# Output projection: transposes of the second normalisation one step later, copies by half, residuals loaded one tile ahead

## The chip, the cores and the metric

The kernel runs on one core of a Trainium2 chip. The metric is the device time of one execution in microseconds (us), as the median of several runs; lower is better. One more execution was recorded by the profiler, and all rows shown here come from it. PE is TensorE (matmul; PEld is its weight load), DVE is VectorE, ACT is ScalarE, POOL is GpSimd, SP is SyncE, which issues all the DMAs here.

## The reference

One transformer block with modulation (adaLN): 2048 tokens, width 1024, 32 heads of 32, feed-forward width 3584.

```python
h = _layernorm(x) * (1 + ca) + sa
x = x + ga * _A_ref(h, wq, wk, wv, wo, beta)     # 4 segments of 512 tokens, softmax attention + a memory
h = _layernorm(x) * (1 + cb) + sb
x = x + gb * _B_ref(h, w_gate, w_up, w_down)     # (gelu(h @ w_gate) * (h @ w_up)) @ w_down
```

The change sits where the first half ends and the second begins: `o @ wo`, the addition of the residual `x`, and the second layer normalisation with its scale `1 + cb` and shift `sb`, whose result is wanted transposed (width on the partitions) for the feed-forward products.

## The kernel before, in words

**Stages.** An opening and 33 attention steps (until about 990 us), the output projection (from 937 us within the last two attention steps, alone until 1151.5 us), the gate and up products (`gate_up`, two passes over the tokens, 28 column blocks each) and the down product (`down`).

**Precision.** Every product of the projection and the feed-forward is done in three matmuls with operands cut into a high part (ACT copy into fp32r) and a low part (DVE or POOL subtraction): high x high, low x high, high x low. Such cuts (L201 to L208 for the attention output, L821 and L823 for the feed-forward's operands) are the most frequent work of ACT, DVE and POOL around the change.

**Output projection (`project`, L678 to L697; `projections`, L739 to L772).** Blocks of (segment s, half nb of the 1024 output columns) run in the order (0,0), (1,0), (0,1), (1,1), (2,0), (3,0), (2,1), (3,1). A block has four tiles of 128 tokens by 512 columns. A tile loads its residual from `x` (L684), issues 24 matmuls into one of two PSUM slots (`mm_ps`, L690), and after them DVE adds PSUM and residual (L694) and SP stores the sum to `x1_d` (L695). So the second tile after a tile can only start when that tile's addition has read its PSUM slot.

**Where a residual lives (`x_tile`, L665).** In the first six blocks it is one of four quarters of a buffer `xr`, taken in turn; in the blocks (2,1) and (3,1) it is half of a tile of the ring `raw`, which has four slots and serves operand loads as well: `a_part` (L951) takes two slots of it for its odd columns, `b_part` (L1018, L1019) two for each column block of the gate and up weights.

**Steps and sides.** After every six matmuls `project` yields, and `step()` gives each entry of the list `sides` one or two turns: load and cut the next segment's attention output (`load_hT`), normalise (`norm_tiles`), cut the first feed-forward operands (`a_part`, `b_part`). A tile of the projection is four such steps. Within a step the engines get the work in the order of the list. PE, DVE, ACT and POOL keep the order in which the program names their instructions. SP keeps it too during attention, that is for the block (0,0) and the first tiles of (1,0); later the planner orders SP's DMAs by its own estimate of when they are ready.

**Second normalisation (`norm_tiles` with name "b", `norm_steps`).** Eight tiles of 128 tokens by 1024 (segments 0 and 1) start five steps apart from the block (0,1) on. Counted from its own start, a tile is loaded from `x1_d` at step 0 (L238); at step 5 DVE takes its statistics (L216 to L221) and POOL the power -1/2 (L222); at step 7 DVE forms the shift (L227) and ACT scales the tile in place (L229); at steps 9 and 10 its two halves are transposed by PE, four 128 x 128 blocks into one PSUM tile (`turn`, L250), and the four blocks are copied out with scale and shift, two by ACT (L258) and two by DVE (L256) in turn, into one buffer that SP sends to `h2_d` (L259). With five steps between tiles, step 10 of one tile is step 5 of the next, and the turn comes first in it. The other eight tiles (segments 2 and 3) are normalised in the same way within the first pass of `gate_up`, with `wait=6` and spacings of their own (L271 to L287).

**First users.** `a_part((1, 6, 2, 7))` reads `h2_d` from the 11th step of the block (3,0) on, and cuts in (2,1); `a_part((5, 4))` follows in (3,1). The first product of `gate_up` runs at 1151.5 us.

Of the kernel before, what the change touches and what calls it, by code (L numbers as in the profile page):

```python
# [19 lines left out]
P = 128  # L20
# [9 lines left out]
L = 512  # L30
# [6 lines left out]
def block_kernel(ctx: ExitStack, tc: tile.TileContext, x, c, wmod, wq, wkv, wo, beta, wg, wu, wd, out):  # L37
    nc = tc.nc
# [37 lines left out]
    def raw_tile(name):  # L76
        return big.tile([P, 1024], F32, name=name, tag="raw", bufs=4)
# [4 lines left out]
    def tmp_tile(name):  # L82
        return big.tile([P, L], F32, name=name, tag="tmp", bufs=4)
# [5 lines left out]
    def mm_ps(name):  # L89
        return psum.tile([P, L], F32, name=name, tag="mm", bufs=2)  # L90

    def s_ps(name):
        return psum.tile([P, L], F32, name=name, tag="s", bufs=5)
# [118 lines left out]
    def norm_stats(halves, name, behind=False):  # L212
        st = cs([P, 2, 6], "st" + name, tag="st", bufs=4)
        mv = cs([P, 2], "mv" + name, tag="mv", bufs=4)
        for h in range(2):
            i = nc.vector.bn_stats(st[:, h], halves[h])  # L216
            if behind:
                hold(i)
        nc.vector.bn_aggr(mv, st.rearrange("p a b -> p (a b)"))
        rs = cs([P, 1], "rs" + name, tag="rs", bufs=4)  # L220
        nc.vector.tensor_scalar_add(rs, mv[:, 1:2], EPS)  # L221
        nc.gpsimd.tensor_tensor(rs, rs, mhalf[:, :1], op=ALU.pow)  # L222
        return mv, rs

    def norm_scale(ts, mv, rs, name):
        mr = cs([P, 1], f"mr{name}", tag="mr", bufs=4)
        nc.vector.tensor_scalar(mr, mv[:, 0:1], rs, -1.0, op0=ALU.mult, op1=ALU.mult)  # L227
        for t in ts:
            nc.scalar.activation(t, t, AF.Identity, bias=mr, scale=rs)  # L229

    def norm_tiles(src, dst, segs, jscale, jshift, name, tiles=range(4), wait=0, get=raw_tile, more=[]):

        toks = [s * L + i * P for s in segs for i in tiles] + more
        dv = dst.rearrange("(k p) t -> p k t", p=P)
        xs = {}
        def load(q):
            xs[q] = (raw_tile if name == "b" and not wait and q % 3 == 2 else get)(f"n{name}{toks[q]}")
            nc.sync.dma_start(xs[q], src[toks[q]:toks[q] + P, :])  # L238

        def stat(q):  # L240
            t = xs[q]
            xs[q, "s"] = norm_stats([t[:, :L], t[:, L:]], f"{name}{toks[q]}")

        def turn(q, h):
            t, tok = xs[q], toks[q]
            ps = s_ps(f"tp{name}{tok}_{h}")
            hh = tmp_tile(f"ht{name}{tok}_{h}")
            for k in range(4):
                kt = 4 * h + k
                nc.tensor.transpose(ps[:, k * P:(k + 1) * P], t[:, kt * P:(kt + 1) * P], ident)  # L250
            for k in range(4):
                kt = 4 * h + k
                sl = slice(k * P, (k + 1) * P)
                sc, sh = (modT[:, 8 * j + kt:8 * j + kt + 1] for j in (jscale, jshift))
                if h if name == "a" else k % 2:
                    nc.vector.tensor_scalar(hh[:, sl], ps[:, sl], sc, sh, op0=ALU.mult, op1=ALU.add)  # L256
                else:
                    nc.scalar.activation(hh[:, sl], ps[:, sl], AF.Identity, bias=sh, scale=sc)  # L258
            send_h = lambda: nc.sync.dma_start(dv[:, 4 * h:4 * h + 4, tok:tok + P], hh.rearrange("p (k t) -> p k t", t=P))  # L259
            if wait:  # L260
                later(3, send_h)
            elif name == "a":
                xs[q, h] = send_h
            else:
                send_h()

        if name == "a":
            return load, lambda q: stat(q), lambda q: norm_scale([xs[q]], *xs.pop((q, "s")), f"a{toks[q]}"), turn, lambda q, h: xs.pop((q, h))()
        return norm_steps(toks, xs, load, turn, name, wait)

    def norm_steps(toks, xs, load, turn, name, wait):  # L271
        if wait:
            for q in range(len(toks)):
                load(q)
                for _ in range(wait):
                    yield
                t, nm = xs[q], f"{name}{toks[q]}"
                mv, rs = norm_stats([t[:, :L], t[:, L:]], nm)
                for _ in range(3):
                    yield  # L280
                norm_scale([t], mv, rs, nm)
                for _ in range(wait - 2):
                    yield
                for h in range(2):
                    turn(q, h)
                    yield
            return  # L287
        for at in range(5 * len(toks) + 7):
            for q in range(len(toks)):
                k = at - 5 * q  # L290
                if k == 0:
                    load(q)
                elif k == 5:
                    t, nm = xs[q], f"{name}{toks[q]}"
                    st = norm_stats([t[:, :L], t[:, L:]], nm)
                elif k == 7:
                    norm_scale([t], *st, nm)
                elif k in (9, 10):
                    turn(q, k - 9)
            yield  # L300

    def norm_seg(s, halves):
# [34 lines left out]
    for n in range(2):  # L337
        k = p1.tile([P, 4, L], F32R, name=f"ks{n}")
# [326 lines left out]
    def x_tile(name):  # L665

        if xrs[0] is None:
            return raw_tile(name)[:, :L]
        xrs[1] += 1
        return f32(xrs[0][:, xrs[1] // 2 % 2, xrs[1] % 2 * L:(xrs[1] % 2 + 1) * L])  # L670
# [5 lines left out]
        return r  # L676

    def project(s, todo):  # L678
        for i, nb in todo:
            ws = wot[nb]  # L680
            tok = s * L + i * P
            fs = slice(nb * L, (nb + 1) * L)
            xr = x_tile(f"xr{s}_{nb}_{i}")
            nc.sync.dma_start(xr, x[tok:tok + P, fs])  # L684
            ps = mm_ps(f"y{s}_{nb}_{i}")
            for g in range(G):
                w = ws[g // 2].rearrange("p h (k m) -> p h k m", m=L)
                hi, lo = oh[s][g]
                for a, b in ((0, hi), (0, lo), (1, hi)):
                    nc.tensor.matmul(ps, b[:, i * P:(i + 1) * P], w[:, a, g % 2],  # L690
                                     start=(g == 0 and a == 0 and b is hi), stop=(g == G - 1 and a == 1))
                if g % 2 == 1 and g < G - 1:
                    yield
            nc.vector.tensor_add(xr, ps, xr)  # L694
            store = lambda tok=tok, fs=fs, xr=xr: nc.sync.dma_start(x1_d[tok:tok + P, fs], xr)  # L695
            later(2, store) if waiting[0] else store()
            yield  # L697
# [4 lines left out]
    def later(n, f):  # L702

        late.append([n, f])
# [34 lines left out]
    def projections():  # L739
        def block(s, *nbs):  # L740
            for _ in project(s, [(i, nb) for i in range(4) for nb in nbs]):
                step()
                yield
# [934 lines left out]
```

## Time and profile before

| | |
|---|---|
| time, median of 3 runs | 2776.51 us (2775.17 to 2778.23) |
| the profiled execution | 2774.08 us |
| its span, first to last instruction | 2772.4 us |
| mean granted TensorE clock | 0.995 |
| PE busy | 2725.8 us (98%) |
| PEld, DVE, ACT, POOL busy | 82%, 57%, 43%, 32% |
| HBM traffic | 372.79 MB read, 211.81 MB written |
| share of L690 (output projection) in the chain that ended last | 4% |

How to read it: a row of a group gives line, engine, operation and tiles, then the count and the times; buffer numbers are left out of names. "a <- b: t, n, m" among the waits says that a waited for b for t us in n times, m at the longest. In a list in order of time the columns are start, length, engine, line, operation, count, and in brackets the idle time of the engine before it with what ended it. A wait for several things is put down to the one that came last; where that one had long been done, it was another, often a DMA. `nb` are the tiles of the second normalisation, `tpb` their transposes in PSUM, `htb` the copies, `xr` a residual, `y` the projection's sums, `ra`, `rb` and `A` the feed-forward's left operands, `rg`, `ru` and `B` its right ones.

### The profile page before, as it was taken

The numbers are of one execution on the slowest core, as the hardware profiler recorded it, in microseconds if no ns is written. First come the engines' busy times: TensorE is split into PE (matmuls) and PEld (weight loads), VectorE is DVE, ScalarE is ACT, GpSimd is POOL, SyncE is SP. The second block draws the span as 40 slices with busy tenths as digits, with TensorE's granted clock in tenths as the row PEclk, the third lists the DMA queues.
The fourth block names the chain that finished last, engine by engine and source line by source line (L and its number), as shares of the span: only waits on it lengthen the run. The fifth ranks groups of instructions, "written<-read, shape, count | busy, mean of one in ns | idle before, by whom it ended". The sixth has DMA issues, their size and how long they took to land.

```text
span 2772.4 us, 43014 instructions
## 1 busy us (share of the span) xinstructions
PE 2725.8 (98%) x14748; PEld 2286.4 (82%) x14748; DVE 1568.4 (57%) x3519; ACT 1204.0 (43%) x2806; POOL 888.9 (32%) x1448
## 2 busy tenths in 40 slices
PE   7999999999999999999999999999999999999999
PEld 6798888888888777778888878888888888888887
DVE  7677667766676735655555445333433244475456
ACT  5677777776767624334322323111111033233323
POOL 5333334533333533344555552444351000000000
PEclk8999999999999999999999999999999999999999
DMA  6455444435443558778898778999999687796563
GB/s 228 135 147 151 113 145 137 134 100 147 121 130 100 149 183 273 243 293 302 321 340 322 267 267 279 341 362 362 353 361 329 215 303 264 259 307 207 179 206 127
DMA packets 244890, 637.77 MB, mean 230 GB/s; under 512 B 24768, under 2 KB 49344, under 8 KB 244672
## 3 DMA queue, kind: packets, MB, share of 16 engines
q1 hardware_dynamic: 244672, 635.03, 67.5%
q8 instruction: 116, 1.90, 0.3%
q14 instruction: 102, 0.84, 0.1%
HBM read 372.79 MB, written 211.81 MB: 211 GB/s over the span
## 4 chain that ended last, share of the span: by engine, by line
PE 89%; DVE 4%; issue 2%; POOL 2%; DMA 1%; ACT 1%; SPq 0%; POOLq 0%; ACTq 0%; DVEq 0%
PE f L1107 35%; PE y L1306 19%; PE kv L367 12%; PE q L373 6%; PE y L690 4%; PE S L524 3%; PE T L615 3%; PE O L627 3%; PE num L583 1%; PE M L566 1%; PE tpb L250 0%; POOL t L827 0%; PE R L633 0%; PE kT L401 0%; PE kv L496 0%
## 5 line engine op out<-in xcount | busy, mean ns | idle before, releaser
L1107 PE MATMUL f<-A,B 128*128 128x512 f32 x4704 | 1075.0, 390 | 3.6 <-DVE c L1127 1.5
L1107 PEld LDWEIGHTS f<-A,B 128*128 128x128 f32 x4704 | 880.8, 188 | 190.8 <-DVE c L1119 2.8
L1306 PE MATMUL y<-B,L 128*128 128x512 f32 x2352 | 533.3, 389 | 0.0
L1306 PEld LDWEIGHTS y<-B,L 128*128 128x128 f32 x2352 | 441.4, 188 | 91.7
L528 ACT ACTIVATE sj<-sj,mm 128x384 f32<-128x384 f32 (+3 forms) x512 | 281.4, 552 | 52.6 <-DVE mm L526 52.0
L526 DVE CUSTOM_DVE_ANT_0 sj<-S,mask 128x384 f32<-128x384 f32 (+3 forms) x512 | 227.9, 488 | 109.7 <-PE S L524 85.5
L618 POOL TENSOR_SCALAR_AFFINE_SELECT pt<-pt 128x128 f32<-128x128 f32 x512 | 165.3, 345 | 295.0 <-ACT pt L617 288.4
L821 ACT ACTIVATE L<-X 128x512 fp32r<-128x512 f32 x168 | 105.8, 630 | 258.6 <-PE y L1306 167.9
L617 ACT ACTIVATE pt<-T 128x256 f32<-128x256 f32 (+3 forms) x512 | 182.0, 445 | 66.0 <-PE T L615 58.8
L367 PE MATMUL kv<-w,hhh 128*128 128x256 f32 x1024 | 199.6, 285 | 0.0
L823 DVE TENSOR_TENSOR L<-X,L 128x512 fp32r<-128x512 f32 x168 | 116.0, 692 | 146.2 <-ACT L L821 146.1
L1130 ACT ACTIVATE g<-g 128x512 f32<-128x512 f32 x56 | 35.3, 631 | 339.9 <-DVE g L1129 339.9
L358 POOL TENSOR_TENSOR w<-r,w 128x256 fp32r<-128x256 f32 x180 | 133.1, 771 | 155.3 <-ACT w L352 153.7
L367 PE MATMUL kv<-w,hha 128*128 128x256 f32 x896 | 177.0, 285 | 0.0
L1046 POOL TENSOR_TENSOR rw<-rw,gbb 128x256 f32<-128x256 f32 x112 | 91.6, 853 | 247.4 <-DMA rw<-wd 166.5
L367 PEld LDWEIGHTS kv<-w,hhh 128*128 128x128 f32 x1024 | 164.8, 191 | 1.4 <-issue 0.4
L367 PEld LDWEIGHTS kv<-w,hha 128*128 128x128 f32 x896 | 145.6, 191 | 2.0 <-issue 0.8
L367 PE MATMUL kv<-w,hlh 128*128 128x256 f32 x512 | 144.7, 283 | 0.0
L690 PE MATMUL y<-wo,hho 128*128 128x512 f32 x384 | 125.7, 394 | 1.7 <-DVE xr L694 1.7
L367 PE MATMUL kv<-w,hla 128*128 128x256 f32 x448 | 126.9, 283 | 0.0
L1123 ACT ACTIVATE g<-f 128x512 f32<-128x512 f32 x56 | 33.5, 598 | 206.5 <-PE f L1107 206.5
L615 PE MATMUL T<-qs,ks 128*128 128x256 f32 (+2 forms) x512 | 108.3, 334 | 7.5 <-DVE qs L543 4.6
(244 smaller groups left out, 4215.4 us busy)
## 6 DMA issues: line engine op xcount, KB each, us to landing
bc_d<-B SPq DMA_DIRECT2D x189, 512.0 KB, 5.4
B<-bc_d SPq DMA_DIRECT2D x189, 512.0 KB, 5.4
B<-wc_d SPq DMA_DIRECT2D x112, 512.0 KB, 3.8
hid_d<-g SPq DMA_DIRECT2D x56, 512.0 KB, 4.3
wc_d<-T SPq DMA_DIRECT2D x56, 512.0 KB, 7.0
X<-hid_d SPq DMA_DIRECT2D x112, 256.0 KB, 4.9
wr<-gd_d SPq DMA_DIRECT2D x84, 256.0 KB, 4.0
ks<-kh SPq DMA_DIRECT2D x64, 256.0 KB, 3.6
```

The source lines that it names most:

```text
L358: nc.gpsimd.tensor_sub(w[:, 1, c], r[:, c], f32(w[:, 0, c]))
L367: nc.tensor.matmul(ps, b[:, sl], w[:, a], start=(kt == 0 and a == 0 and b is hi), stop=(kt == KT - 1 and a == 1), **kw)
L373: nc.tensor.matmul(ps, w[:, a], b, start=(kt == 0 and a == 0 and b is hi), stop=(kt == KT - 1 and a == 1), **kw)
L526: nc.vector.tensor_tensor_reduce(out=sj[:, :nv], in0=ps[:, :nv], in1=mask[:, L - nv:], scale=-1.0, scalar=3.4e38, op0=ALU.add, op1=ALU.min ...
L528: nc.scalar.activation(sj[:, :nv], sj[:, :nv], AF.Exp, bias=mm[:, j, i:i + 1], scale=-1.0, accum_out=ll[:, i, j:j + 1])
L615: nc.tensor.matmul(ps[:, :nn], ks[:, j, kc * P:(kc + 1) * P], qs[:, j, L - nn:], start=True, stop=True)
L617: nc.scalar.activation(pt, ps[:, nn - n:nn], AF.Exp)
L618: nc.gpsimd.affine_select(pt[:, :P], pt[:, :P], pattern=[[1, P]], compare_op=ALU.is_ge, fill=0.0, base=0, channel_multiplier=-1)
L690: nc.tensor.matmul(ps, b[:, i * P:(i + 1) * P], w[:, a, g % 2], start=(g == 0 and a == 0 and b is hi), stop=(g == G - 1 and a == 1))
L823: eng.tensor_sub(lo[:, k], src[:, k], f32(hi)[:, k])
L1107: nc.tensor.matmul(ps, B[m, i][:, a, kt * P:(kt + 1) * P], A[p, i, kt][b], start=(start and kt == 0 and a == 0 and b == 0), stop=(kt == 3 ...
L1306: nc.tensor.matmul(banks[t], ops[k][:, y, t * P:(t + 1) * P], B[slots[k]][:, x], start=(i not in (2, 4, 3) and j == 0 and x == 0 and y == ...
```

## The change

Three edits:

- In `turn`, which half goes to which engine: the four copies of half 0 are all done by ACT, the four of half 1 all by DVE. Before, that held for the first normalisation (name "a") only, and for "b" even blocks went to ACT and odd ones to DVE. The "b" tiles within `gate_up` go through the same lines.
- In `norm_steps`, the branch without `wait`: the halves are turned at steps 10 and 11 instead of 9 and 10, and the loop is one step longer.
- In `project`, the load of a residual: at a block's start the loads of its first two tiles are asked for, and at the start of each further tile that of the tile after it. Before, each tile asked for its own.

```diff
-                if h if name == "a" else k % 2:
+                if h:
                     nc.vector.tensor_scalar(hh[:, sl], ps[:, sl], sc, sh, op0=ALU.mult, op1=ALU.add)
                 else:
                     nc.scalar.activation(hh[:, sl], ps[:, sl], AF.Identity, bias=sh, scale=sc)
...
-        for at in range(5 * len(toks) + 7):
+        for at in range(5 * len(toks) + 8):
...
-                elif k in (9, 10):
-                    turn(q, k - 9)
+                elif k in (10, 11):
+                    turn(q, k - 10)
...
     def project(s, todo):
-        for i, nb in todo:
+        ahead = []
+
+        def load(i, nb):
+            ahead.append(x_tile(f"xr{s}_{nb}_{i}"))
+            nc.sync.dma_start(ahead[-1], x[s * L + i * P:s * L + (i + 1) * P, nb * L:(nb + 1) * L])
+
+        load(*todo[0])
+        for n, (i, nb) in enumerate(todo):
             ws = wot[nb]
             tok = s * L + i * P
             fs = slice(nb * L, (nb + 1) * L)
-            xr = x_tile(f"xr{s}_{nb}_{i}")
-            nc.sync.dma_start(xr, x[tok:tok + P, fs])
+            xr = ahead.pop()
+            if n + 1 < len(todo):
+                load(*todo[n + 1])
             ps = mm_ps(f"y{s}_{nb}_{i}")
```

With the turn at steps 10 and 11, step 10 of one tile is still step 5 of the next; now the first half is turned in it, ahead of the next tile's statistics in the program, and the second half one step after them.

## The prediction

> **What bounds the kernel now.** I read the page first, then the table by stretch, then who waited for whom on PE, then the lists in order of time around single waits.
>
> ```profile
> PE 2725.8 (98%) x14748; PEld 2286.4 (82%) x14748; DVE 1568.4 (57%) x3519; ACT 1204.0 (43%) x2806; POOL 888.9 (32%) x1448
> ```
> ```profile
> 1000.00:1100.00 100.00, 95.75 (x448) 77.58 (x448) 46.97 (x101) 36.68 (x64) 26.62 (x36) 1.00 0.72 233
> 1100.00:1152.00 52.00, 50.26 (x222) 41.09 (x221) 30.80 (x45) 12.92 (x23) 11.97 (x12) 1.00 0.85 276
> 1200.00:1400.00 200.00, 197.07 (x891) 160.50 (x890) 116.30 (x195) 77.27 (x137) 103.50 (x130) 1.00 0.84 306
> ```
> PE sets the end: it is busy for 2725.8 of the 2772.4 us, and everything that the change touches can only pay by filling PE's gaps. The columns of the table are length, busy time of PE, PEld, DVE, ACT, POOL, the granted clock, DMA share, GB/s. In the output projection (until 1151.5 us) PE idles 4.3 and 1.7 us in the first two rows, and 2.9 us in the 200 us of feed-forward in which the second half of the tiles is normalised. That is all there is to win. Who holds PE there:
>
> ```profile
> PE tpb L250 <- ACT nb L229: 4.3, 7, 1.1
> PE y L690 <- DVE xr L694: 1.7, 1, 1.7
> PE f L1107 <- DVE c L1119: 1.0, 3, 0.6
> ```
> Seven times the transposes wait for the scaling of their tile, once a projection waits for a PSUM slot that an old tile's residual addition (L694) still holds; in the feed-forward stage products wait for VectorE evictions such as L1119.
>
> **The transposes, part one.** One of the seven waits, on PE, then DVE and ACT:
>
> ```profile
> 1046.02 0.60 PE L250 MATMUL tpb<-ident,nb 128*128 128x128 f32 x4
> ...
> 1051.70 0.39 PE L690 MATMUL y<-ks,hho 128*128 128x512 f32 x1
> 1052.84 0.66 PE L250 MATMUL tpb<-ident,nb 128*128 128x128 f32 x4 [0.76 <-ACT nb L229]
> ...
> 1054.49 0.39 PE L690 MATMUL y<-ks,hho 128*128 128x512 f32 x1
> 1054.73 0.60 PE L250 MATMUL tpb<-ident,nb 128*128 128x128 f32 x4
> ```
> ```profile
> 1048.13 0.41 DVE L256 TENSOR_SCALAR htb<-tpb,modT 128x128 f32<-128x128 f32 x1 [0.53 <-ACT htb L258]
> 1048.46 1.28 DVE L216 BATCH_NORM_STATS2 stb<-nb 128x6 f32<-128x512 f32 x2
> 1050.10 0.69 DVE L694 TENSOR_TENSOR xr<-y,xr 128x512 f32<-128x512 f32 x1
> 1050.70 0.68 DVE L208 TENSOR_TENSOR hlo<-ro,hho 128x512 fp32r<-128x512 f32 x1
> 1051.30 0.21 DVE L227 TENSOR_SCALAR mrb<-mvb,rsb 128x1 f32<-128x1 f32 x1
> ```
> ```profile
> 1051.55 1.24 ACT L229 ACTIVATE nb<-nb,mrb,rsb 128x1024 f32<-128x1024 f32 x1 [2.92 <-DVE mrb L227]
> ```
> Read as a loop: the second half of one tile is transposed at 1046.02; its copies ping-pong between ACT and DVE until 1048.54; only then does DVE, in its order, take the next tile's statistics, POOL the power, DVE the mean and ACT the scaling, done at 1052.79, 6.77 us after 1046.02. PE would come to the next tile's first half at 1051.70 + 0.24 = 1051.94, 5.92 us after (0.24 is the undisturbed step from a projection to a transpose, 1054.49 to 1054.73). So it waits: 1052.84 - 1051.94 = 0.90 us, the shown idle of 0.76 and 0.14 beside it. Seven such: 4.3 + 7 x 0.14 = **5.3 us**; the shown 4.3 is the lower end.
>
> The change alters this loop twice. First, with the transposes one step later (six matmuls, some 1.4 us: the halves start 1054.73 - 1052.84 = 1.89 us apart, of which the four transposes take about 0.5), the next tile's statistics stand in the step of the *first* half, one ahead of the second. Second, copies by half take DVE out of the first half, so the statistics no longer wait for a transpose at all. The longest wait, 1.1 + 0.14, is shorter than the step alone. What is late next: the second half's four copies now stand ahead of the mean on DVE. From the second half's transposes on: 0.66 for these, 4 x 0.41 of copies, in the worst alignment one cut (0.68) and one residual addition (0.69), the mean 0.21, the scaling 1.24: 5.1 us, against 5.92 on PE. Some 0.3 to 0.6 of hand-overs still fit. I take **-5.3 us**; ends 0 (the loop stays) and -5.3.
>
> **Copies by half.** Nothing is added: eight copies of a tile remain four on each engine.
>
> ```profile
> L258 ACT ACTIVATE htb<-tpb,modT x64: 437/458/461, 1027.9 to 1365.8; 128x128 f32<-128x128 f32 x64
> L256 DVE TENSOR_SCALAR htb<-tpb,modT x64: 399/410/413, 1028.4 to 1366.3; 128x128 f32<-128x128 f32 x64
> ...
>   DVE htb L256: 38.9, 51
> ```
> The last row: DVE sat idle 38.9 us in 51 waits for ACT's copy of the same PSUM tile, so the two take turns although they write different columns. By half, an engine needs 4 x 0.41 to 0.46 = 1.6 to 1.8 us without a partner. In the feed-forward stage the same chain stands ahead of evictions:
>
> ```profile
> 1281.03 16.62 PE L1107 MATMUL f<-A,B 128*128 128x512 f32 x72 [0.63 <-DVE c L1119]
> 1368.18 22.05 PE L1107 MATMUL f<-A,B 128*128 128x512 f32 x96 [0.87 <-DVE c L1125]
> ```
> ```profile
> 1279.17 0.41 DVE L256 TENSOR_SCALAR htb<-tpb,modT 128x128 f32<-128x128 f32 x1 [0.53 <-ACT htb L258]
> 1279.68 0.69 DVE L823 TENSOR_TENSOR B<-rg,B 128x512 fp32r<-128x512 f32 x1
> 1280.30 0.68 DVE L1119 TENSOR_TENSOR c<-f,c 128x512 f32<-128x512 f32 x1
> ...
> 1366.31 0.41 DVE L256 TENSOR_SCALAR htb<-tpb,modT 128x128 f32<-128x128 f32 x1 [0.53 <-ACT htb L258]
> ```
> Before 1281.03 about one hand-over (0.53) goes, so some 0.5 of the 0.63. Before 1368.18 the cut between the halves comes first and all four copies (1.64) after it, where now two and a hand-over stand (2 x 0.41 + 0.53), so it stays or grows by 0.3. On balance **-0.4 us** over the stage; ends -1.5 (both waits) and +1.5 (ACT's four in a row push an eviction as far again the other way).
>
> **The residual, loaded one tile ahead.** Only one wait hangs on it:
>
> ```profile
> 1118.93 0.79 SPq L951 DMA_DIRECT2D ra<-h_d  x2
> ...
> 1120.87 0.83 SPq L684 DMA_DIRECT2D xr<-x  x1
> ```
> ```profile
> xr<-x SPq DMA_DIRECT2D x1, 256.0 KB, 7.7
> ```
> ```profile
> 1123.88 0.68 DVE L969 TENSOR_TENSOR s<-ra,s 128x512 f32<-128x512 f32 x1
> 1128.68 0.69 DVE L694 TENSOR_TENSOR xr<-y,xr 128x512 f32<-128x512 f32 x1 [4.12 <-PE y L690]
> 1129.29 0.68 DVE L823 TENSOR_TENSOR A<-ra,A 128x512 fp32r<-128x512 f32 x1
> ...
> 1134.28 0.68 DVE L694 TENSOR_TENSOR xr<-y,xr 128x512 f32<-128x512 f32 x1
> ```
> ```profile
> 1127.31 0.39 PE L690 MATMUL y<-ks,hho 128*128 128x512 f32 x1
> 1129.43 0.50 PE L690 MATMUL y<-wo,hho 128*128 128x512 f32 x1 [1.74 <-DVE xr L694]
> ```
> The idle of 4.12 is booked on PE, but the load issued at 1120.87 needs 7.7 us and lands at 1128.6, just ahead of the addition: it is the load. The Trainium skill, "DMA: Bandwidth & Descriptors", section "Anatomy of one DMA — SWDGE (gpsimd) path", fits one DMA (of another issue path) with about 2.0 us plus its bytes at 436 GB/s, which makes an estimate of 2.6 us for these 256 KB. By that it would have landed at 1123.5, the wait would have another cause, and the edit would be worth nothing; the row of 7.7 us speaks against the fit in this stretch. PE loses 2.12 - 0.24 = **1.9 us**. The new load is asked for a tile earlier, but takes a slot of the four-slot ring `raw`, which until 1118.9 belongs to operand tiles and residuals in flight. So I expect it some 2 us earlier, ahead of the two operand loads of 1118.93 instead of behind them; even with 7.7 us to landing its addition is then over by 1127.3, when PE comes for the slot (1127.31 + 0.24), and DVE is free from 1124.56. What is late next: from 1129.29 to 1134.96 DVE does one operand column and then the next tile's addition, 5.67 us, which must end by 1129.43 - 1.9 + 5.5 = 1133.0 (a tile is four steps); it may start up to 1127.3, and the operand's ScalarE cut is done at 1125.9 (row below). Slack 1.4 us, and a load of 256 KB more ahead of it costs about 1 us at the 276 GB/s of this stretch. I take **-1.9**; ends 0 and -1.9.
>
> ```profile
> 1125.23 0.63 ACT L821 ACTIVATE A<-ra 128x512 fp32r<-128x512 f32 x1 [2.46 <-DMA ra<-h_d]
> ```
> Costed at nothing: the other 31 residual loads, as many and as large as before, only earlier on SP. On SP each moves ahead of stores and tile loads, and waits for its slot:
>
> ```profile
> SPq L684 <- DMA x_d<-xr: 25.7, 11, 4.8
> ```
> ```profile
> 1043.47 0.33 SPq L238 DMA_DIRECT2D nb<-x_d  x1
> 1057.20 1.28 DVE L216 BATCH_NORM_STATS2 stb<-nb 128x6 f32<-128x512 f32 x2
> ```
> Behind it wait the tiles to normalise; one is issued some 14 us before use (last two rows), so 4.8 us more is covered. Without that cover each such wait would come back as a wait of L216.
>
> **Sum.** -5.3 - 0.4 - 1.9 = **-7.6 us**. The profiled execution took 2774.08 us (span 2772.4 and 1.7 around it), 2.4 under the median of the runs shown; the sum is against its own gaps, and its result there is 2766.5. Moved to the median, 2776.51 - 7.6 = **2768.9 us**. A measurement of this kernel can tell about 0.2%, 5.6 us, from no change: the forecast is just beyond that.
>
> **Rivals.** (1) *The residual arrives no earlier*, since its slot comes free only with the operand tiles and DMA is 0.85 busy there: then 5.7 is won, **2770.8**. For it: the slot; against: the load now stands ahead of two 512 KB loads. (The fit of the Trainium skill, above, would give the same time for another reason.) (2) *The loop closes again*: the four DVE copies of the second half, a cut and an addition fall together more often than I think, and half of the 5.3 stays: -4.9, **2771.6**. (3) *The ring turns against it*, the slower case: residuals now hold a `raw` slot one tile longer, and the last pair of operand loads (1118.93) gets the slot of the residual asked for ahead of it. That one is added at 1125 to 1126, done 0.7 later, and stored in about the 7.7 us that its load took, so the operand loads go out up to 15.4 us late (1134.3); past the slack of 1.4 us each us is PE's, at the second tile of the last block: +14.0 on the -7.6, **2782.9**. It decides at an operand load issued after about 1128 in the old time, where the gain is gone. Against: today the pair found its two slots free at 1118.93, before this residual asked for one.
>
> **Chances.** Forecast 58%, rival 1 14%, rival 2 and mixtures of both 20%, rival 3 8%. Rivals 1 and 2 lie about the bound of 2771.0, so of their 34% some 12 count as faster: faster 70%, same 22%, slower 8%. The range runs from 2765.5 (both eviction waits gone too, and 1.5 us of spread of the runs) to 2775.5 (a small part of the loop gain only); rival 3 and little else lies outside.
>
> **What would show it.** Right: no PE wait for nb L229; the waits of DVE htb on ACT htb gone; statistics (L216) starting before the second half's copies; the residual of 1120.87 issued ahead of the operand pair, and no wait of PE on L694. Wrong: a tpb wait on nb with mrb released late; operand loads (L951) later than 1119 by more than 1.4 us against the projection; new waits of f on A or c.

## The result and the profile after

The changed kernel takes **2764.85 us** (median of 5 runs, 2762.92 to 2765.96), the kernel before 2776.54 beside it (5 runs, 2775.17 to 2778.23). The ratio is 0.9956, with a 95% interval of 0.9941 to 0.9971: 11.7 us faster, where 7.6 were forecast, and 0.65 us below the lower end of the range. The profiled execution of after took 2764.85 us (span 2763.1), 9.2 less than that of before.

The page's engine line, and the same three stages as before, moved to where they now lie (length, then busy time of PE, PEld, DVE, ACT, POOL, clock, DMA share, GB/s):

```profile
PE 2725.3 (99%) x14748; PEld 2288.7 (83%) x14748; DVE 1559.1 (56%) x3519; ACT 1201.1 (43%) x2806; POOL 890.6 (32%) x1448
```
```profile
1000.00:1094.00 94.00, 94.00 (x447) 77.89 (x447) 43.84 (x101) 34.85 (x64) 26.09 (x36) 1.00 0.75 250
1094.00:1146.00 52.00, 51.84 (x229) 42.64 (x228) 31.34 (x45) 13.31 (x23) 12.02 (x12) 1.00 0.88 266
1192.00:1392.00 200.00, 197.93 (x899) 162.40 (x898) 114.20 (x196) 75.52 (x138) 103.91 (x130) 1.00 0.85 310
```
PE does the same 2725 us of work; what went is idle time. Through the projection with its transposes PE no longer stops at all (94.00 of 94.00; before 95.75 of 100), in the last two blocks it loses 0.16 us. All waits of PE from the last attention steps to the end of the first feed-forward pass (total, times, longest):

```profile
PE T L615 <- ACT pt L617: 2.7, 1, 2.7
PE f L1115 <- DVE c L1133: 0.9, 1, 0.9
PE f L1115 <- DVE c L1135: 0.9, 2, 0.5
PE O L627 <- POOL pt L618: 0.8, 1, 0.8
PE f L1115 <- DVE c L1127: 0.3, 1, 0.3
PE y L698 <- DVE xr L702: 0.2, 1, 0.2
```
(Lines behind `project` are 8 higher than before; L1115 is the old L1107, L702 the old L694.) No transpose waits for `nb`, and the wait for a residual has shrunk from 1.7 to 0.2. The loop of a tile now runs like this on DVE, and then on ACT:

```profile
1044.01 1.28 DVE L216 BATCH_NORM_STATS2 stb<-nb 128x6 f32<-128x512 f32 x2
...
1046.51 1.36 DVE L256 TENSOR_SCALAR htb<-tpb,modT 128x128 f32<-128x128 f32 x4
...
1048.38 0.21 DVE L227 TENSOR_SCALAR mrb<-mvb,rsb 128x1 f32<-128x1 f32 x1
```
```profile
1044.56 1.51 ACT L258 ACTIVATE htb<-tpb,modT 128x128 f32<-128x128 f32 x4 [0.67 <-ACT hho L201]
...
1048.62 1.24 ACT L229 ACTIVATE nb<-nb,mrb,rsb 128x1024 f32<-128x1024 f32 x1 [2.04 <-DVE mrb L227]
```
The statistics of the next tile start 2.5 us ahead of DVE's copies, not behind them, and the four copies of a half run back to back in 1.36 and 1.51 us. SP in the last two blocks, then the addition of that residual on DVE:

```profile
1112.98 0.33 SPq L683 DMA_DIRECT2D xr<-x  x1
1113.41 1.86 SPq L959 DMA_DIRECT2D ra<-h_d  x2
```
```profile
1118.62 0.68 DVE L702 TENSOR_TENSOR xr<-y,xr 128x512 f32<-128x512 f32 x1
```
The residual stands ahead of the pair of operand loads, as forecast. It landed after 3.1 us (before, behind the pair: 7.7), and its addition (the last row) came without idle time. The 0.2 that is left in the list belongs to the next residual: its load left SP at 1121.23, its addition waited 1.60 us for the transfer (1126.60 on DVE), and PE lost 0.16 us to it.

**Where the time went, by stage.** The same matmul (by its place in PE's order) starts at one time in one trace and at another in the next; the growth of that difference over a stage is what the stage gained. Against the profiled execution of before: -0.3 us in the attention steps, -5.7 in the transposes (1026 to 1098 us of before), -1.7 in the last two blocks (1098 to 1152), **-1.7 in the first feed-forward pass** (1152 to 1373), 0.2 elsewhere; -9.2 together. The remaining 2.5 us of the 11.7 are that this one execution of before was 2.5 us under the median of the five beside it, while that of after is its median.

So two questions: which edit won in the feed-forward pass, where -0.4 had been forecast, and what an execution of before typically loses that its trace didn't show.

### The profile page after: what moved, and what is told of

The parts are those of the page before. It is cut to its first block, busy times and chain, and to the rows that moved or that the text cites. A ratio compares the mean times of both kernels' runs of the same rounds, so it can differ in the third digit from the quotient of the medians.

```text
span 2763.1 us, 42996 instructions
## 1 busy us (share of the span) xinstructions
PE 2725.3 (99%) x14748; PEld 2288.7 (83%) x14748; DVE 1559.1 (56%) x3519; ACT 1201.1 (43%) x2806; POOL 890.6 (32%) x1448
## 4 chain that ended last, share of the span: by engine, by line
PE 91%; DVE 3%; DMA 2%; issue 1%; POOL 1%; ACT 1%; SPq 0%; DVEq 0%; ACTq 0%; POOLq 0%
PE f L1115 36%; PE y L1314 19%; PE kv L367 12%; PE q L373 6%; PE y L698 5%; PE S L524 3%; PE T L615 3%; PE O L627 3%; PE num L583 1%; PE M L566 1%; PE R L633 0%; PE kT L401 0%; PE tpb L250 0%; PE kv L496 0%; DMA bc_d<-B 0%
## 5 line engine op out<-in xcount | busy, mean ns | idle before, releaser
L1115 PE MATMUL f<-A,B 128*128 128x512 f32 x4704 | 1074.2, 390 | 2.8 <-DVE c L1135 1.3
L1115 PEld LDWEIGHTS f<-A,B 128*128 128x128 f32 x4704 | 881.3, 188 | 188.8 <-DVE c L1135 2.6
L618 POOL TENSOR_SCALAR_AFFINE_SELECT pt<-pt 128x128 f32<-128x128 f32 x512 | 166.0, 348 | 295.2 <-ACT pt L617 288.7
```

What stands on the lines that cost most here:

```text
L618: nc.gpsimd.affine_select(pt[:, :P], pt[:, :P], pattern=[[1, P]], compare_op=ALU.is_ge, fill=0.0, base=0, channel_multiplier=-1)
L1115: nc.tensor.matmul(ps, B[m, i][:, a, kt * P:(kt + 1) * P], A[p, i, kt][b], start=(start and kt == 0 and a == 0 and b == 0), stop=(kt == 3 ...
```

## The experiments

**The theory** when they began: three separate gains (loop of transposes, late residual, feed-forward evictions), the last one mis-sized. **The rival**: the early loads do something more, outside the last two blocks. First the three edits in all eight combinations (the kernel before itself among them), each over five rounds:

```diff
 half   -                if h if name == "a" else k % 2:
        +                if h:
 later  -                elif k in (9, 10):
        +                elif k in (10, 11):     # and one step more in the loop
 ahead  -            xr = x_tile(...); nc.sync.dma_start(xr, x[...])
        +            xr = ahead.pop(); load(*todo[n + 1])
```

The kernel before once more. 

> The kernel before, unchanged, to see how far one execution of it stands for the others: the changed kernel won 9.3 us in the pair of profiled spans, but 11.7 us between the medians. Theory 1 (the profiled execution of before was simply one of its faster ones): the median comes out between 2775 and 2778, ratio 1.000 within 0.001, and this new profile is again up to 3 us away from the median, with the same gaps: tpb behind nb 4 to 5 us in 7 waits, y behind xr 1 to 3 us in one or two waits. Theory 2 (the gaps themselves are longer in ordinary executions, since the waits on DMAs vary): a profile of a slower execution shows y behind xr, or products behind late operands, 2 to 3 us longer than the first one did.

half alone. 

> Only the copies by half (transposes and residuals as before). Theory 1 (the loop from one tile's second half to the next tile's first half sets the seven waits): the statistics still stand behind the second half's copies, which take 0.66 + 4 x 0.41 = 2.3 us in place of 2.5, so the loop shortens by 0.2 us and each wait by as much: about -1.5 us there, and about -1.7 us in the feed-forward stage, where the changed kernel's offset grew by that much: -3 us in all, 2773.5. Rival (the copies taking turns were the whole of the loop, the step of the transposes nothing): the waits of tpb on nb are gone, -7 us, 2769.5. Rival (the feed-forward gain comes from the shift of DMAs against PE, not from the copies): the feed-forward stage shows no gain, -1.5 us in all.

later alone. 

> Only the transposes one step later (copies taking turns, residuals as before). Theory 1 (statistics must be freed from the copies too): DVE still copies two blocks of the first half ahead of the statistics and two of the second half ahead of the mean, so the scaling ends some 5.9 to 7.2 us after the second half's transposes against PE's 5.9: about half of the waits stays, -2.5 to -3.5 us, and none of the feed-forward gain: 2773.5. Rival (the step alone frees the loop): tpb waits gone, -5.5 us, 2771.0.

ahead alone. 

> Only the residual loaded one tile ahead. Theory 1 (the wait of PE for the residual addition at the start of the last block is its load): that wait goes from 1.7 to under 0.3 us, -1.9 us, 2774.6; the seven waits on nb and the feed-forward stage are as before. Theory 2 (in ordinary executions the late residual costs more than the profile showed): -3 to -5 us, 2772.5. Rival (the slot in the ring raw decides, not the asking): -0.3 us, nothing.

half and later. 

> Copies by half and transposes one step later, residuals as before. Theory A (the two edits of the transposes carry nearly all of the change; each alone took 3 to 4 us out of the projection because the loop's waits are partly the same): the waits of tpb on nb are gone, -5.7 us there, -1.9 us in the feed-forward stage as in half_only, and the wait for the late residual stays near 0.7 to 1.0 us: -8 us against before, within 1 us of the whole change. Rival B (the load ahead is worth its 1.9 us in company though not alone): this kernel comes out 2 us or more behind the whole change measured beside it.

half and ahead. 

> Copies by half and residuals one tile ahead, transposes at their old steps. Theory A: as half_only within 1 us (-4 to -6 us), four or more waits of tpb on nb of 0.2 to 0.7 us still there, feed-forward stage 1.9 us shorter than before. Rival B (the load ahead pays in company): -6.5 us or more.

later and ahead. 

> Transposes one step later and residuals one tile ahead, copies taking turns. Theory A: as later_only within 1 us (-4 to -6 us), since the load ahead alone measured nothing; feed-forward stage as before; the wait of y on xr moves but does not vanish for good. Rival B (the load ahead pays once the projection's waits are gone): -6.5 us or more.

All three. 

> The changed kernel, unchanged, with more executions. Theory A (executions of either kernel scatter over some 8 us, by the clock's start and by waits in attention that the change does not touch; the 11.7 us between the first medians is partly that scatter): -8 to -9.5 us against before on the same chip. Rival (the change is worth 11.7 us and the pair of profiles understates it): -11 to -12.5 us. In the profile: no tpb wait on nb, y on xr at most 0.5 us.

Measured (us; "difference" is that of the means to before on the same chip; the four columns behind it come from the one profiled execution: change of the stage against before's trace, as above, and the longest wait of PE for an O, L627 in the last attention steps, 1.8 in before's trace):

| kernel | median | ratio, 95% interval | difference | transposes | last two blocks | feed-forward pass | wait of O |
|---|---|---|---|---|---|---|---|
| before_again | 2775.93 | 1.0002 [0.9993, 1.0011] | +1.1 | 0.0 | -0.9 | +0.1 | 3.5 |
| half_only | 2770.23 | 0.9983 [0.9974, 0.9992] | -5.4 | -3.2 | -0.8 | -1.8 | 2.5 |
| later_only | 2769.95 | 0.9982 [0.9973, 0.9991] | -5.1 | -4.3 | -0.8 | +0.2 | 2.3 |
| ahead_only | 2774.40 | 1.0002 [0.9994, 1.0011] | +0.1 | 0.0 | +1.0 | +0.1 | 0.8 |
| half_later | 2769.64 | 0.9975 [0.9966, 0.9984] | -7.5 | -5.7 | -0.5 | -1.8 | 3.3 |
| half_ahead | 2765.38 | 0.9969 [0.9956, 0.9981] | -9.9 | -3.2 | -2.2 | -1.8 | 0.8 |
| later_ahead | 2768.19 | 0.9974 [0.9965, 0.9983] | -7.4 | -4.2 | -2.2 | +0.2 | 0.8 |
| after_again | 2764.50 | 0.9963 [0.9950, 0.9975] | -11.6 | -5.7 | -2.2 | -1.8 | 0.8 |

What follows, column by column. *Transposes*: each of the two edits opens most of the loop by itself, and together they gain less than the sum (5.7, not 3.2 + 4.3), since they remove the same waits; what each leaves:

```profile
PE tpb L250 <- ACT nb L229: 1.4, 4, 0.7
```
```profile
PE tpb L250 <- ACT nb L229: 0.7, 2, 0.5
```
The first is half_only, the second later_only; with both no such line is left. *Feed-forward*: -1.7 to -1.8 in each kernel with copies by half, about 0 in each without: it is that edit alone. *Last two blocks*: with the early load and either other edit they are 1.7 to 2.2 us shorter than in before's trace; without the early load 0.5 to 0.9 shorter, so some 0.8 to 1.7 go to the load itself. Alone it lost 1.0 there, in two waits for residuals of the last block (0.4 and 2.2 us), against what the shorter wait of O gained. *Wait of O*: 2.3 to 3.5 us in all executions without the early load but the profiled one of before (1.8), 0.8 at the longest in all with it. That stage had not been in the forecast.

Several expectations missed. half alone and later alone won more in the transposes than their theories had it (3.2 and 4.3 us, where 1.5 and 2.5 to 3.5 were expected). ahead alone was to win 1.9 us and won nothing. For half and later, half and ahead, later and ahead and the whole change, the theories held that the early load adds about 1 us at most in company; it added 4 us to half and later on the same chip, and the rival fits in all four.

**Why the early load reaches O.** Rows of before on SP, POOL and PE, and the time from issue to landing of the four loads of line L111 (the late half of the output weights):

```profile
975.25 0.33 SPq L684 DMA_DIRECT2D xr<-x  x1
...
976.16 1.96 SPq L111 DMA_DIRECT2D ro<-wo  x4
```
```profile
983.62 4.04 POOL L181 TENSOR_TENSOR wo<-ro,wo 128x256 fp32r<-128x256 f32 x4 [0.78 <-ACT wo L176]
987.62 2.01 POOL L618 TENSOR_SCALAR_AFFINE_SELECT pt<-pt 128x128 f32<-128x128 f32 x4
```
```profile
988.95 1.14 PE L627 MATMUL O<-pt,vx 128*32 128x128 f32 x8 [1.81 <-POOL pt L618]
```
```profile
DMA to landing us min/median/max: 4.9/6.2/7.3
```
And of after:

```profile
972.11 0.44 SPq L683 DMA_DIRECT2D xr<-x  x1
...
976.13 1.81 SPq L111 DMA_DIRECT2D ro<-wo  x4
```
```profile
983.01 3.40 POOL L181 TENSOR_TENSOR wo<-ro,wo 128x256 fp32r<-128x256 f32 x4 [0.67 <-ACT wo L176]
986.37 3.00 POOL L618 TENSOR_SCALAR_AFFINE_SELECT pt<-pt 128x128 f32<-128x128 f32 x4
```
```profile
988.94 0.90 PE L627 MATMUL O<-pt,vx 128*32 128x128 f32 x6 [0.82 <-POOL pt L618]
```
```profile
DMA to landing us min/median/max: 3.9/6.2/7.4
```
The weights are asked for at the same time (976.1). In before a residual load of 256 KB leaves SP 0.9 us ahead of them, for its slot came free only then; with the early load it leaves 4.0 us ahead. The first of the four weight tiles then lands after 3.9 instead of 4.9 us. Each tile is scaled on DVE, cut on ACT, and its low part is subtracted on POOL in four pieces (L181), and behind these in POOL's order stand the masks of the attention (L618) that PE's O needs. Over the eight kernels of the table and the two of the first comparison, the first landing and the wait of O go together: without the early load 4.9 and 1.8; 5.7 and 2.3; 6.0 and 2.5; 6.3 and 3.3; 6.9 and 3.5; with it 3.9 to 5.1, and 0.8 at the longest. With the early load a second, smaller wait stands ahead of that one (0.1 to 0.2 us; 0.75 in later_ahead, where the weights landed after 5.1), so PE wins less than the row falls: from the first O to the next matmul of the projection, 12.6 us in before, 11.9 in after.

This is still only a correlation. Two kernels split the early load by where the residuals live, and two take POOL's subtractions out of the masks' way, each over five rounds on one chip (a third one; the kernels of the table ran on two others).

**Early load in the first six blocks only** (half and later kept):

```diff
+        early = xrs[0] is not None
+        if early: load(*todo[0])
...
+            if not early: load(i, nb)
             xr = ahead.pop()
+            if early and n + 1 < len(todo): load(*todo[n + 1])
```


> Copies by half and transposes a step later stay; the residual is loaded a tile ahead only in the first six blocks, whose slots are the four of xr, and as before in the last two, whose slots are those of raw. Theory: the early load pays mostly in the last attention steps, since there the residual load of the next tile no longer stands 0.9 us ahead of the late output weights on SP; their subtractions on POOL then come earlier, and the masks behind them, on which PE waits for O, too. Then the wait of O on pt is 0.8 us (half_later 3.3), the wait of PE on xr in the last block stays (0.5 to 1.7), and the time is 1.5 to 2.5 us below half_later's 7.5 under before: a mean of 9 to 10 us under before, with little scatter. Rival: all that the early load is worth is the late residual of the last block; then O waits 1.8 to 3.5 us as without it, and the time stays at 7.5 under before.

Measured: median 2764.68 us, mean 9.1 under before, ratio 0.9966 [0.9952, 0.9980]. PE's waits beside that of T, which is 2.7 us in every kernel (lines 12 higher than in before, here and in the next kernel):

```profile
PE y L702 <- DVE xr L706: 1.9, 1, 1.9
PE O L627 <- POOL pt L618: 0.8, 1, 0.8
```

**Early load in the last two blocks only**:

```diff
+        early = xrs[0] is None
```


> The other half of the same split: the residual is loaded a tile ahead only in the last two blocks, whose slots are those of raw. Theory: the wait of PE on xr falls to 0.2, which is worth 0.6 to 1.7 us against half_later, and the wait of O on pt stays between 1.8 and 3.5: a mean of 8 to 9.5 us under before, scattered over some 8 us. Rival: the whole gain of the early load sits here, and the mean is 11 to 12 under before.

Measured: median 2765.96 us, mean 8.4 under before, ratio 0.9971 [0.9959, 0.9982]. PE's waits, again without that of T:

```profile
PE O L627 <- POOL pt L618: 3.3, 1, 3.3
PE y L702 <- DVE xr L706: 0.4, 1, 0.4
```
The two waits follow the two halves of the edit crosswise: the first six blocks bring O down to 0.8 and leave the residual's 1.9; the last two bring that to 0.4 and leave O at 3.3. The times (9.1 and 8.4 under before, 11.6 with both) fit, but do not decide: single executions scatter by about 2 us (standard deviation) in these two, where little scatter and some 8 us were expected, and their intervals overlap with that of half_later (7.5). It is the rows of the waits that refute the forecast's view that the whole of the early load's gain is the late residual. The first of the two kernels moves all 24 loads of the first six blocks; the one in front of the weights was not moved by itself.

**The late weights' subtractions on VectorE** (half and later, no early load):

```diff
-  split_w(gated(rs[k - 1], 1), w.rearrange(...))
+  split_w(gated(rs[k - 1], 1), w.rearrange(...), nc.vector)
```


> Copies by half and transposes a step later, residuals loaded as before; the low parts of the late output weights (four splits) are subtracted on VectorE, one instruction each, and not by four instructions each on POOL. Theory: what makes O wait is those subtractions in POOL's order ahead of the masks, so the wait of O on pt goes without any earlier load: from 3.3 to under 0.5 us, the scatter goes with it, and the mean is 9 to 10.5 under before. Rival: the masks are late because ScalarE's exponentials are (they stand behind ScalarE's copies of the same weights, which stay); then O still waits 1 to 3 us, on pt of L617 instead of L618, and the mean stays at 7 to 8 under before.

Measured: median 2766.55 us, mean 9.1 under before, ratio 0.9968 [0.9956, 0.9979]. PE's waits until the end of the projection:

```profile
PE y L690 <- DVE xr L694: 2.8, 2, 2.1
PE T L615 <- ACT pt L617: 2.7, 1, 2.7
```
No wait of O is left, though the first weight tile landed late here too (5.9 us). So the masks waited for POOL's own queue, not for ACT's exponentials; the wait of T on these is the same 2.7 us as in before. The gain is a little short of the theory's middle. A residual, not loaded early here, cost PE 2.1 us (1122.79). The other 0.7 (998.60) is the price of the edit: the addition there starts at 997.86, straight behind the moved subtractions and the last attention work on DVE, and half_later has no wait there. The scatter was to go and did not (2762.37 to 2768.24), and by its interval alone the time does not tell theory from rival.

**Both**, the whole change with that edit:

> The whole change, and the late output weights' subtractions on VectorE as well. Theory: the early load has left 0.8 us of the O wait, and that goes: 12 to 13 under before (after_again 11.6). Rival: VectorE's subtractions of about 1.3 us stand ahead of the projection's additions and of R, and what POOL no longer holds up VectorE does: 10.5 to 11.6 under before.

Measured: median **2760.93 us** (2759.47 to 2763.75, 5 runs), mean 13.8 under before, ratio 0.9951 [0.9939, 0.9964]. Its waits of PE over the same stretch as the list of after above:

```profile
PE T L615 <- ACT pt L617: 2.7, 1, 2.7
PE f L1115 <- DVE c L1133: 0.9, 1, 0.9
PE f L1115 <- DVE c L1135: 0.9, 2, 0.5
PE f L1115 <- DVE c L1127: 0.3, 1, 0.3
```
The rows of O and of the residual are gone and the others unchanged. It has the lowest median of all kernels run; against before it is 14 us, but its interval and that of the change (0.9950 to 0.9975 in after_again) overlap, so that it beats the change is likely, and shown in the trace only by the two rows that are gone.

## Why the prediction was too small

- **Transposes, -5.3 forecast: right.** -5.7 in both executions of the change. The rows of the waits show 4.3, so PE did lose more around each than its row, as reckoned; nothing new came late. The mark to look for, statistics ahead of the second half's copies, is there. That the loop closes again for half of the gain (rival 2) did not happen.
- **Copies by half in the feed-forward pass, "on balance -0.4": the failed step.** -1.7 measured, and -1.8 in the others with that edit. The mechanism was named rightly (the copies' turn-taking stands in DVE's order ahead of evictions), but only two waits were priced, one as gone and one, the 0.87 before 1368.18, as staying (0.93 in after). The edit removed or shortened others too. Two that the prediction didn't price, and what DVE does ahead of the second, from before:

```profile
1227.78 4.38 PE L1107 MATMUL f<-A,B 128*128 128x512 f32 x18 [0.73 <-DVE c L1127]
1260.12 15.26 PE L1107 MATMUL f<-A,B 128*128 128x512 f32 x66 [0.17 <-DVE c L1119]
```
```profile
1256.89 0.41 DVE L256 TENSOR_SCALAR htb<-tpb,modT 128x128 f32<-128x128 f32 x1 [0.94 <-ACT htb L258]
1257.83 0.41 DVE L256 TENSOR_SCALAR htb<-tpb,modT 128x128 f32<-128x128 f32 x1 [0.53 <-ACT htb L258]
1258.34 1.12 DVE L823 TENSOR_TENSOR B<-rg,B 128x512 fp32r<-128x512 f32 x1
1259.39 0.68 DVE L1119 TENSOR_TENSOR c<-f,c 128x512 f32<-128x512 f32 x1
```
  and what DVE does there in after, and the first of the two waits there:

```profile
1247.64 1.37 DVE L256 TENSOR_SCALAR htb<-tpb,modT 128x128 f32<-128x128 f32 x4 [2.97 <-PE tpb L250]
1248.92 1.02 DVE L831 TENSOR_TENSOR B<-rg,B 128x512 fp32r<-128x512 f32 x1
1249.87 0.68 DVE L1127 TENSOR_TENSOR c<-f,c 128x512 f32<-128x512 f32 x1
```
```profile
1219.61 4.39 PE L1115 MATMUL f<-A,B 128*128 128x512 f32 x18 [0.37 <-DVE c L1135]
```
  In before the hand-overs of 0.94 and 0.53 stand ahead of the eviction L1119, which is over at 1260.07, just ahead of PE's start at 1260.12; in after the four copies come without a gap between them, and no wait of PE is left in that place; the one of 0.73 has halved. Matmul by matmul, the gains are 0.34 and 0.35 at 1224 and 1227.8, 0.44 at 1260.1 and 0.72 at 1281.0 (forecast for this one 0.5), with some 0.2 lost at others. The four copies in a row did not push another eviction as far, which had been the end at +1.5.

  The first two gains, 0.7 us together, come by a path that the prediction did not have: no copies stand on DVE just ahead of those evictions. From before, SP and then ACT:

```profile
1214.95 0.37 SPq L259 DMA_DIRECT2D h_d<-htb  x1
1215.37 7.14 SPq L1026 DMA_DIRECT2D bc_d<-B  x6
```
```profile
1219.78 0.63 ACT L821 ACTIVATE B<-t 128x512 fp32r<-128x512 f32 x1 [0.61 <-DMA bc_d<-B]
```
  Six stores of B stand on SP behind the store of the second half's copies, and by the profile it is one of these stores that frees the place of the next B, for which ACT waits 0.61 us. In after these stores start at 1206.66, 1.2 us earlier against PE, ACT's cut follows without a wait (1211.61), and DVE's cut and evictions behind it come 0.7 us earlier against PE. later_only, without copies by half, has the wait of 0.61 again and half_only doesn't have it.
- **The late residual, -1.9 forecast: right in place and mechanism, and in size only against this one trace.** -1.7 and -2.2 in the change; the one wait that was priced gave its 1.9 us (matmul by matmul, at 1129.43 of before), and 0.2 was lost again behind it. But the wait that it removes is 0.7 to 2.1 us, by execution, in the kernels without it. Rival 1 (no earlier) is out: the load stands ahead of the operand pair. Rival 3 (the ring turns against it) shows only in small in the change: the second load of the pair waited 1.1 us for the store of a residual and left SP 1.6 us later against PE than before, which is past the 1.4 named as a sign; the rows show no loss of PE there beyond the 0.16 us above. In ahead_only the last blocks were 1.0 us *slower*, with late residuals again (2.6 us in two waits, against 0.4 at most in the other kernels with the early load in these blocks). The longer of the two is a matter of order on SP: there the residual's load (1136.00) stands behind a store (1134.97), which waits for an addition that is late itself, and behind an operand load (1135.57); in after the same load (1125.44) goes out ahead of both (1127.32 and 1127.92). Why the planner ordered the two programs differently is not shown.
- **"Costed at nothing: the other 31 residual loads": the other failed step.** It asked only who waits behind the moved loads on SP, and found cover. It did not ask which transfer a load stands *ahead of* today, though the same question had been put at 1118.93. One of the 31 stood 0.9 us ahead of the late weights; with the loads of the first six blocks moved, the wait of O is 1 to 2.7 us shorter, by the execution compared with.
- **"The sum is against its own gaps", moved to the median.** In before's own trace O waited 1.8 us, in the five others that load the residuals of the first six blocks as before and subtract on POOL 2.3 to 3.5: in this gap the profiled execution was a lucky one, and understates what there was to win. In the gap of the late residual it was not (1.7 us, against 0.7 to 2.1 in the other six), and as a whole it was ordinary: its 2774.08 us are 1.3 under the mean of the 65 further executions of before that were timed beside the experiments (2771.21 to 2779.64), and the five beside the change were 1.1 over that mean at the median. In two traces a second loss follows the long wait of O: in before_again (3.5 us) and ahead_last_two (3.3) the granted clock fell behind it, in the first like this (length, busy times, then the clock of 0.61):

```profile
992.00:996.00 4.00, 4.00 (x14) 3.25 (x13) 1.12 (x2) 0.00 (x0) 4.00 (x7) 0.61 0.21 72
```
  The 24 matmuls that follow took 6.9 and 6.5 us there, and 5.6 in all other kernels. half_later waited 3.3 us as well and kept a clock of 1.00, so what decides it is not shown. All this, and different speeds of the opening (the first 110 us differ by up to 3.6 us among the profiled executions, whichever edits they have, at granted clocks of 0.86 to 0.95 in this stretch), lie between profile and median; they were not taken apart further.

By the trace alone the sum was -7.6 against -9.2 measured: the difference is 1.3 for the evictions, 0.4 for the transposes and 0.3 for the attention steps, less 0.4 elsewhere.

## What to carry to other kernels

Where a load is moved, look at both sides of it in the queue: what waits behind its new place, and what was waiting behind its old one; the second can be a chain through three engines that the moved transfer itself never touches. Price every wait of a kind, and not only the largest rows, when an edit shortens what stands ahead of all of them. And before a gap of one profiled execution is entered into a sum, ask how far it depends on when a transfer lands; such gaps differ from execution to execution, and removing one gains its typical size and some of the scatter.

## What the runs showed of the hardware

Where the weights landed late, POOL's subtractions became slower as well. Before_again, in which the weights landed last:

```profile
985.43 4.76 POOL L181 TENSOR_TENSOR wo<-ro,wo 128x256 fp32r<-128x256 f32 x4 [3.65 <-ACT wo L176]
```
```profile
986.05 2.88 DVE L675 TENSOR_TENSOR ro<-ro,gab 128x1024 f32<-128x1024 f32 x2
```
ahead_first_six, in which they landed earliest (3.8 us after their issue):

```profile
985.75 2.83 POOL L181 TENSOR_TENSOR wo<-ro,wo 128x256 fp32r<-128x256 f32 x4
```
```profile
988.83 2.54 DVE L675 TENSOR_TENSOR ro<-ro,gab 128x1024 f32<-128x1024 f32 x2
```
The same four subtractions take 2.83 us by themselves and 4.76 beside two DVE multiplications, which take 2.88 instead of 2.54. One by one, two of the four take 1.7 us instead of 0.73, those that begin while a multiplication runs, and the second multiplication takes 1.75 instead of 1.3. The Trainium skill, "SBUF — State Buffer", section "Terms", says that DVE and GpSimd share one pair of ports and that the one who loses it is blocked for the other's whole instruction; the 1.9 us more on POOL, against two multiplications of 1.27 each, agrees with that. Late weights fall into this collision, early ones mostly come ahead of it (in after one of the four is slowed, to 1.31). On the queue, the same skill's "DMA: Bandwidth & Descriptors", section "Queues, rings and completion order", says that an engine takes what one issuer's ring holds in order; the first weight tile's landing at 3.8 to 5.1 us with the residual gone ahead and 4.9 to 6.9 with it just in front agrees.
